# State-exchange attention and a squared-ReLU-like MLP in fp32 on one core: the last batch's state read placed later, and the states' outputs stored by two strided transfers per tile

## The chip, the cores and the metric

The kernel runs on one core of one Trainium2 chip. The metric is the device time of one execution in microseconds (us). A core has TensorE (PE: matmuls; its weight loads are listed as PEld), VectorE (DVE), ScalarE (ACT), GpSimd (POOL) and SyncE (SP). Transfers are issued here from the queues of SP and ACT and carried by 16 DMA engines. Matmul results land in PSUM, everything else on the chip is in SBUF, and both have 128 partitions.

## The reference

Eight batches of eight heads, 512 tokens and 32 states of 64 values each:

```
scores  = x @ state.T / 8;  xread = softmax(scores)  @ state    # tokens read the states
scores2 = state @ x.T / 8;  sread = softmax(scores2) @ x        # states read the tokens
rows = concat(xread, sread) per batch                           # 8 * (512 + 32) = 4352 rows of 512
h = rows @ w_in                                                 # 512 -> 2048
g = h if h >= 1, 0 if h <= -1, else (h + 1)**2 / 4
out = g @ w_out                                                 # 2048 -> 512, fp32
```

In `out`, batch b's rows are 544 b to 544 b + 543: first 512 token rows, then 32 state rows.

## The kernel before

Each matmul of the MLP is made of three: operands are split into a high and a low part, and high·high, low·high and high·low are summed in PSUM. The tokens of a batch never have their `xread` written out: the product of the states with `w_in` (called `sw`, fp32 matmuls, L385) is made per batch and per chunk of 256 of the 2048 hidden columns, so that the first layer is `softmax · sw` (L450 to L452, into PSUM tile `h`). ScalarE and VectorE turn `h` into `g` (L467 to L488), and L526 to L528 sum `g @ w_out` into four PSUM tiles `acc` of 128 tokens. After the start-up, whose order is a table of numbers, the program is a plain loop over `steps` (L812, L876): batches 1 to 7 with eight steps j each, and last a batch numbered 8, which is no batch of tokens but the 256 state rows of all eight batches (two `acc` tiles, four steps).

The change touches two places.

**The first step of a batch (j = 0), L880 to L895.** Behind the previous batch's last products stand, in PE's order: the states' read of the tokens (`read2`, L329: 32 matmuls at L337 into PSUM tile `sr`, from the transposed second softmax `e` and the tokens `xn`), then the `sw` products of seven chunks: 1 and 2 (into two `acc` banks), 3 and 4 (into the two `h` banks), 5 and 6 (two `acc` banks), and 7, for the last batch in the PSUM tile that `sr` uses. `scale2` (L342) is two VectorE operations: L345 normalises `sr` to `rs`, L349 transposes it to `rt`, which SP's queue puts in place for the last batch (L355, 16 small transfers). Then each pair of chunks is split: ScalarE casts the high part (L406, `copy` at L625), and VectorE subtracts to get the low part (L412). The first-layer product of step j = 1 takes chunk 1 and an `h` bank, and an `h` bank is free once the low part of the pair 3, 4 has been read from it.

**The end of the program, `store` (L534).** For batch 8, each `acc` tile t (0 and 1) holds 128 rows: 32 state rows of each of four batches. Tile 0 is copied to SBUF by ScalarE (L541), tile 1 by VectorE (L539). Then four transfers (L548) of 32 rows of 2 KB go out, one per batch, since in `out` the batches' state rows lie 544 rows apart; two are issued from ACT's queue and two from SP's. The last group of products is sorted by tile, so that tile 0's transfers go out while tile 1 is still being summed.

Of the kernel before, what the change touches and what calls it, by code (L numbers as in the profile page):

```python
# [98 lines left out]
def state_exchange_moe(  # L99
# [17 lines left out]
    nc = tc.nc  # L117
    B, P, NT, H, D = x.shape
    S = NT * P
    NS = 32  # L120
# [7 lines left out]
    TOK = S + NS  # L128
# [16 lines left out]
    def ps_mm(name):  # L145
        return ps.tile([P, 2, 512], F32, tag="mm", bufs=1, name=name)
# [30 lines left out]
    def load_xt(b):  # L177
        xt = work.tile([P, 2, NPR, S // 2], F32, tag="xt", bufs=1, name=f"xt{b}")
        for i in range(2):
            nc.sync.dma_start(out=xt[:, i], in_=xt_in[b, i])  # L180
        return xt

    def load_xn(b):
        xn = work.tile([P, NT, H, D], F32, tag="xn", bufs=1, name=f"xn{b}")
        nc.sync.dma_start(out=xn, in_=x[b])
        return [xn[:, t] for t in range(NT)]
# [12 lines left out]
    class Attention:  # L199
# [81 lines left out]
        def rest(self, q):  # L281
            nc.vector.tensor_tensor(
                out=self.atl[:, q], in0=self.zt[:, q], in1=self.ath[:, q].bitcast(F32), op=ALU.subtract
            )
# [76 lines left out]
    def split_tiles(name, home=None):  # L361
        if home:
            both = (rawp if home == "raw" else work).tile([P, 2, 1024], F32R, tag=home, bufs=2 if home == "raw" else 1, name=f"{name}hl")
            return both[:, 0], both[:, 1]
        hi = work.tile([P, 1024], F32R, tag="wh", name=f"{name}h")
        lo = work.tile([P, 1024], F32R, tag="wl", name=f"{name}l")
        return hi, lo
# [5 lines left out]
    def sw_product(items, apart=None, home=None):  # L373

        b, c = items[0]
        if apart:
            banks = [apart(f"sw{b}_{c}_{hh}") for hh in range(2)]
        else:
            pt = ps_mm(f"sw{b}_{c}")
            banks = [pt[:, hh] for hh in range(2)]  # L380
        for i, (bi, ci) in enumerate(items):
            for pr in range(NPR):
                for hh in range(2):
                    rows = slice(hh * 64, hh * 64 + 64)
                    nc.tensor.matmul(  # L385
                        banks[hh][pr * NS:(pr + 1) * NS, i * CI:(i + 1) * CI],
                        lhsT=sb[rows, bi, pr], rhs=w32[ci][rows, pr], start=True, stop=True,
                    )
        w = len(items) * CI
        if b == 0 and c < NH:  # L390
            whole = work.tile([P, 1024], F32, tag="wh", name=f"sw{b}_{c}w").rearrange("p (q f) -> p q f", q=2)[:, :, :w]
            sw_of[b, c] = [(banks[q][:, :w], whole[:, q], None) for q in range(2)]
            chunk[b, c] = whole, None
            return
        wh, wl = (
            v[:, :2 * w].rearrange("p (q f) -> p q f", q=2) for v in split_tiles(f"sw{b}_{c}", home)
        )
        if apart:
            sw_of[b, c] = [(banks[q][:, :w], wh[:, q], wl[:, q]) for q in range(2)]
        else:  # L400
            sw_of[b, c] = [(pt[:, :, :w], wh, wl)]
        for i, item in enumerate(items):
            cols = slice(i * CI, (i + 1) * CI)
            chunk[item] = wh[:, :, cols], wl[:, :, cols]

    def sw_high(b, c, engine="ACT"):  # L406
        for pt, wh, _ in sw_of[b, c]:
            copy(engine, wh, pt)

    def sw_low(b, c):  # L410
        for pt, wh, wl in sw_of[b, c]:
            nc.vector.tensor_tensor(out=wl, in0=pt, in1=wh.bitcast(F32), op=ALU.subtract)  # L412
# [9 lines left out]
    acc = {}  # L422
# [67 lines left out]
    def g1(b, j, split=True):  # L490
        hid = Hidden(b, j)
        for i in range(2):
            hid.product(i)
            hid.relu(i)
            hid.square(i)
            hid.bound(i)
            if i == 0:
                issue("half", b, j)
        if split:
            hid.high()  # L500
            hid.low()
        return hid

    def g2(b, j, half=None):
        n = n_of[b]
        per = S // n
        nt = n // P
        if b not in acc:
            acc[b] = [ps_acc(f"acc{b}_{t}") for t in range(nt)]
        gh, gl = gs[b, j]  # L510
        last = j == NJ // per - 1
        pairs = [(i, t) for i in range(2 * per) for t in range(nt)]
        if last:
            pairs.sort(key=lambda p: p[1])
        if half is not None:
            pairs = pairs[half * len(pairs) // 2:][:len(pairs) // 2]
        for i, t in pairs:
            f = 2 * per * j + i
            oh, ol = wo[f // 2][:, 0, f % 2], wo[f // 2][:, 1, f % 2]
            c0 = (i % per) * n + t * P  # L520
            lh, ll = (v if v is None else v[:, i // per, c0:c0 + P] for v in (gh, gl))
            a = acc[b][t]
            if ll is None:
                nc.tensor.matmul(a, lhsT=lh, rhs=ol, start=f == 0, stop=False)
                continue
            nc.tensor.matmul(a, lhsT=lh, rhs=oh, start=f == 0, stop=False)  # L526
            nc.tensor.matmul(a, lhsT=lh, rhs=ol, start=False, stop=False)  # L527
            nc.tensor.matmul(a, lhsT=ll, rhs=oh, start=False, stop=f == NF - 1)  # L528
            if last and i == 2 * per - 1:
                store(b, t)  # L530
# [3 lines left out]
    def store(b, t):  # L534
        if t == 0:
            outs[b] = rawp.tile([P, NT, DM], F32, tag="raw", name=f"o{b}")
        o = outs[b][:, t]
        if b == B and t % 2:
            nc.vector.tensor_copy(o, acc[b][t])  # L539
        else:  # L540
            nc.scalar.copy(out=o, in_=acc[b][t])  # L541
        if b < B:
            r0 = b * TOK + t * P
            nc.sync.dma_start(out=out[r0:r0 + P, :], in_=o)
        else:
            for i in range(4):
                r0 = (4 * t + i) * TOK + S
                (nc.sync if i % 2 else nc.scalar).dma_start(  # L548
                    out=out[r0:r0 + NS, :], in_=o[i * NS:(i + 1) * NS]
                )  # L550

# [67 lines left out]
    def copy(engine, out, src):  # L621
        if engine == "DVE":
            nc.vector.tensor_copy(out, src)
        else:
            nc.scalar.copy(out=out, in_=src)  # L625
# [28 lines left out]
    atts = {}  # L654

    def att_start(b, half=None):
        if half != 1:
            atts[b] = Attention(b)
        atts[b].scores(half)
# [138 lines left out]
    for word in GROUPS.split():  # L798
        c, n = word.split(".")
# [16 lines left out]
    def later(place, b, j, *items):  # L816
        for f, *a in items:
            background.setdefault((place, b, j), []).append((f, a))

    def issue(place, b, j):  # L820

        for f, a in background.get((place, b, j), ()):
            f(*a)
# [46 lines left out]
    for j in range(NJ // 2 - 1):  # L870
        later("half", B, j, (wi_split, 2 * j + 2))
        later("mid", B, j, (wi_split, 2 * j + 3))

    with guard:
        plan.emit(warm)
        for i, (b, j) in enumerate(steps):  # L876
            prior = steps[i - 1] if i else (0, NJ - 1)
            hid = g1(b, j, split=j or b == B)
            issue("mid", b, j)
            if j == 0 and b < B:  # L880
                g2(*prior, 0)
                hid.high()
                hid.low()
                g2(*prior, 1)
                atts[b].read2()
                sw_product([(b, 1), (b, 2)], ps_acc)
                sw_product([(b, 3), (b, 4)], ps_h)
                sw_product([(b, 5), (b, 6)], ps_acc, "xn")
                atts[b].scale2()
                if b + 1 < B:  # L890
                    att_start(b + 1)
                sw_product([(b, 7), (b + 1, 0)][:B - b], ps_acc if b + 1 < B else None, "raw")
                for c in (1, 3, 5, 7):
                    sw_high(b, c)
                    sw_low(b, c)  # L895
            else:
                g2(*prior)
            if j == 1 and b + 2 < B:
                loaded["xt", b + 2] = load_xt(b + 2)
            issue("end", b, j)  # L900
            if j == 6 and b + 1 < B:
                loaded["xn", b + 1] = load_xn(b + 1)
        g2(*steps[-1])
# [43 lines left out]
```

## Time and profile before

| | us |
|---|---|
| median of 3 runs | 640.0 (639.96 to 640.21) |
| the profiled execution's own time | 640.42 |
| its span, first to last instruction | 638.6 |
| PE busy in it | 628.7 |
| DVE / ACT busy in it | 359.6 / 370.1 |

The profiled execution took 0.4 us more than the median, and 1.8 us of its time lie outside the span. In the views, times are from the span's start. A line of a timeline gives start, length, engine, source line, operation, tiles written and read, and in brackets how long the engine was idle before and what ended that. "x2" and the like count instructions; an fp32 matmul of L337 or L385 shows as two. A DMA line on SPq or ACTq is the issuing, not the transfer; "to landing" is the time from issue to arrival.

### The profile page before, as it was taken

How to read it: one execution, taken by the hardware profiler on the slowest of the kernel's cores; microseconds unless marked ns; L12 is line 12 of the kernel's file. 1: busy time of each engine (PE TensorE's matmuls, PEld its weight loads, DVE VectorE, ACT ScalarE, POOL GpSimd, SP SyncE). 2: the span in 40 equal slices, each digit the busy share in tenths (PEclk: the TensorE clock that was granted, in tenths of full speed). 3: DMA queues.
4: the chain of work that ended last, by engine and by line, in shares of the span. 5: the costliest groups of instructions: out<-in, count | busy, mean ns of one | idle time of the engine just before them, and what ended most of it. 6: DMA issues, size and time to landing. Idle time of an engine off the chain costs nothing.

```text
span 638.6 us, 10431 instructions
## 1 busy us (share of the span) xinstructions
PE 628.7 (98%) x4286; PEld 505.0 (79%) x4286; DVE 359.6 (56%) x536; ACT 370.1 (58%) x539; POOL 0.8 (0%) x7
## 2 busy tenths in 40 slices
PE   7999999999999999999999999999999999999997
PEld 2577787888788887888788887888788878888896
DVE  5999957664565536553555536653555544335431
ACT  5999767545755556555755556555655555454641
POOL 0000000000000000000000000000000000000000
PEclk9999999999999999999999999999999999999999
DMA  8996022412222212011212112011202110000101
GB/s 328 422 371 229 13 70 84 107 28 69 70 69 30 73 50 88 9 26 67 70 67 34 67 67 72 12 32 57 71 1 34 66 69 5 0 1 1 66 1 33
DMA packets 52190, 48.38 MB, mean 76 GB/s; under 512 B 42288, under 2 KB 42416, under 8 KB 49200
## 3 DMA queue, kind: packets, MB, share of 16 engines
q1 hardware_dynamic: 51808, 47.40, 22.7%
q8 instruction: 33, 0.54, 0.4%
q10 hardware_dynamic: 336, 0.33, 0.2%
q14 instruction: 13, 0.11, 0.1%
HBM read 34.08 MB, written 8.91 MB: 67 GB/s over the span
## 4 chain that ended last, share of the span: by engine, by line
PE 89%; ACT 5%; DVE 3%; DMA 1%; issue 1%; SPq 0%; ACTq 0%; DVEq 0%
PE acc L526 18%; PE acc L528 18%; PE acc L527 18%; PE h L450 10%; PE h L451 10%; PE h L452 10%; PE sw L385 4%; PE sr L337 1%; DMA raw_i<-in_moe_w_in_dram 1%; ACT raw_i L580 1%; PE sc L227 1%; ACT raw_o L580 1%; DVE w L592 1%; ACT raw_i L572 1%; ACT u L467 1%
## 5 line engine op out<-in xcount | busy, mean ns | idle before, releaser
L526 PE MATMUL acc<-wo,gh 128*128 128x512 f32 x544 | 212.0, 390 | 0.0
L528 PE MATMUL acc<-wo,gl 128*128 128x512 f32 x544 | 211.8, 389 | 0.1
L527 PE MATMUL acc<-wo,gh 128*128 128x512 f32 x544 | 211.7, 389 | 0.0
L467 ACT ACTIVATE u<-h,half 128x512 f32<-128x512 f32 x136 | 93.3, 689 | 170.3 <-PE h L452 167.7
L474 DVE SCALAR_TENSOR_TENSOR u<-u,h 128x512 f32<-128x512 f32 x136 | 92.8, 687 | 169.0 <-ACT u L471 169.0
L488 DVE TENSOR_TENSOR gl<-u,gh 128x1024 fp32r<-128x1024 f32 x68 | 83.3, 1225 | 74.9 <-ACT gh L625 74.9
L526 PEld LDWEIGHTS acc<-wo,gh 128*128 128x128 f32 x544 | 102.1, 188 | 22.2 <-issue 1.2
L528 PEld LDWEIGHTS acc<-wo,gl 128*128 128x128 f32 x544 | 102.1, 188 | 22.0 <-DVE gl L488 0.7
L527 PEld LDWEIGHTS acc<-wo,gh 128*128 128x128 f32 x544 | 102.1, 188 | 21.1
L625 ACT CAST gh<-u 128x1024 fp32r<-128x1024 f32 x68 | 71.4, 1050 | 41.7 <-DVE u L474 41.6
L471 ACT ACTIVATE u<-u 128x512 f32<-128x512 f32 (+1 forms) x128 | 84.4, 660 | 4.0
L385 PE MATMUL sw<-w,sb 64*32 64x256 f32 x1024 | 32.2, 378 | 2.0 <-DVE w L592 2.0
L385 PEld LDWEIGHTS sw<-w,sb 64*32 64x32 f32 x1024 | 20.0, 106 | 12.9 <-DVE w L592 3.8
L541 ACT COPY o<-acc 128x512 f32<-128x512 f32 x33 | 19.1, 587 | 15.3 <-PE acc L528 15.3
L450 PE MATMUL h<-ath,sw_3h 128*128 128x512 f32 x64 | 25.0, 391 | 0.0
L452 PE MATMUL h<-atl,sw_3h 128*128 128x512 f32 x64 | 24.9, 389 | 0.0
L451 PE MATMUL h<-ath,sw_3l 128*128 128x512 f32 x64 | 24.9, 389 | 0.0
L450 PE MATMUL h<-ath,sw_1h 128*128 128x512 f32 x60 | 24.3, 404 | 0.5 <-DVE sw_3l L412 0.5
L451 PE MATMUL h<-ath,sw_1l 128*128 128x512 f32 x60 | 23.5, 392 | 0.0
L452 PE MATMUL h<-atl,sw_1h 128*128 128x512 f32 x60 | 23.3, 389 | 0.0
L450 PE MATMUL h<-ath,sw_5hl 128*128 128x512 f32 x56 | 21.8, 389 | 0.0
L451 PE MATMUL h<-ath,sw_5hl 128*128 128x512 f32 x56 | 21.8, 389 | 0.0
(174 smaller groups left out, 702.1 us busy)
## 6 DMA issues: line engine op xcount, KB each, us to landing
xt<-in_xt_dram SPq DMA_DIRECT2D x16, 512.0 KB, 4.2
raw_i<-in_moe_w_in_dram SPq DMA_DIRECT2D x8, 1024.0 KB, 7.7
raw_o<-in_moe_w_out_dram SPq DMA_DIRECT2D x8, 1024.0 KB, 10.6
out_dram<-o SPq DMA_DIRECT2D x32, 256.0 KB, 2.1
xn<-in_x_dram SPq DMA_DIRECT2D x7, 1024.0 KB, 4.9
e<-eb SPq DMA_DIRECT2D x112, 32.0 KB, 2.0
srT<-rt SPq DMA_DIRECT2D x128, 4.0 KB, 1.7
xn<-in_x_dram SPq DMA_DIRECT2D x2, 512.0 KB, 5.0
```

The source lines that it names most:

```text
L385: nc.tensor.matmul(banks[hh][pr * NS:(pr + 1) * NS, i * CI:(i + 1) * CI], lhsT=sb[rows, bi, pr], rhs=w32[ci][rows, pr], start=True, stop=True,
L450: nc.tensor.matmul(o, lhsT=wh[:, k, sl], rhs=ah[:, k], start=first, stop=False)
L451: nc.tensor.matmul(o, lhsT=wl[:, k, sl], rhs=ah[:, k], start=False, stop=False)
L452: nc.tensor.matmul(o, lhsT=wh[:, k, sl], rhs=al[:, k], start=False, stop=last)
L467: nc.scalar.activation(out=self.u[:, i], in_=self.hs[i], func=AF.Relu, scale=0.5, bias=half)
L471: nc.scalar.activation(out=u, in_=u, func=AF.Square)
L474: nc.vector.scalar_tensor_tensor(out=self.u[:, i], in0=self.u[:, i], scalar=1.0, in1=self.hs[i], op0=ALU.min, op1=ALU.max,)
L488: nc.vector.tensor_tensor(out=gl, in0=self.u, in1=gh.bitcast(F32), op=ALU.subtract)
L526: nc.tensor.matmul(a, lhsT=lh, rhs=oh, start=f == 0, stop=False)
L527: nc.tensor.matmul(a, lhsT=lh, rhs=ol, start=False, stop=False)
L528: nc.tensor.matmul(a, lhsT=ll, rhs=oh, start=False, stop=f == NF - 1)
L625: nc.scalar.copy(out=out, in_=src)
```

## The change

First, a new function `stretch(b)` holds the first step's `sw` work. For batches 1 to 6 it makes what stood there before. For batch 7 the read of the second softmax comes behind the products of the pairs 1, 2 and 3, 4; then the split of the pair 1, 2 is issued, then `scale2`, then the products of 5, 6 and 7, then the other splits. Second, batch 8's tiles are both copied by ScalarE, and each tile goes out in two transfers instead of four: each covers 64 rows of the SBUF tile, which are two batches of 32 rows in `out`, 544 rows apart. One is issued by ACT, one by SP.

```diff
-        if b == B and t % 2:
-            nc.vector.tensor_copy(o, acc[b][t])
-        else:
+        if b < B:
             nc.scalar.copy(out=o, in_=acc[b][t])
...
-        else:
-            for i in range(4):
-                r0 = (4 * t + i) * TOK + S
-                (nc.sync if i % 2 else nc.scalar).dma_start(
-                    out=out[r0:r0 + NS, :], in_=o[i * NS:(i + 1) * NS]
-                )
+            return
+
+        rows = out.rearrange("(b r) c -> b r c", r=TOK)[4 * t:4 * t + 4, S:S + NS]
+        nc.scalar.copy(out=o, in_=acc[b][t])
+        for i, queue in enumerate((nc.scalar, nc.sync)):
+            queue.dma_start(out=rows[2 * i:2 * i + 2], in_=o[2 * i * NS:2 * (i + 1) * NS])
...
+    def stretch(b):
+        def rest(*chunks):
+            for c in chunks:
+                sw_high(b, c)
+                sw_low(b, c)
+
+        final = b + 1 == B
+        if not final:
+            atts[b].read2()
+        sw_product([(b, 1), (b, 2)], ps_acc)
+        sw_product([(b, 3), (b, 4)], ps_h)
+        if final:
+            atts[b].read2()
+            rest(1)
+            atts[b].scale2()
+            sw_product([(b, 5), (b, 6)], ps_acc, "xn")
+            sw_product([(b, 7)], None, "raw")
+            rest(3, 5, 7)
+            return
...
-                atts[b].read2()
-                sw_product([(b, 1), (b, 2)], ps_acc)
-                sw_product([(b, 3), (b, 4)], ps_h)
-                sw_product([(b, 5), (b, 6)], ps_acc, "xn")
-                atts[b].scale2()
...
+                stretch(b)
```

On PE, in batch 7, the 32 matmuls of L337 move behind the 32 matmuls of the first two pairs. On VectorE, in the same place, this stood before (`rs` and `rt` are `scale2`'s tiles, `sw_1l` the low part of the pair 1, 2, `sw_3l` that of 3, 4, whose PSUM tiles are the `h` banks):

```order
L488 TENSOR_TENSOR gl_0_4689<-u_0_4650,gh_0_4688 128x1024
L345 TENSOR_TENSOR rs_4800<-sr_4708,r_7_4390 128x128
L349 STREAM_TRANSPOSE rt_4802<-rs_4800 128x128
L412 TENSOR_TENSOR sw_1l<-sw_1_0_4741,sw_1h 128x512
L412 TENSOR_TENSOR sw_1l<-sw_1_1_4742,sw_1h 128x512
L412 TENSOR_TENSOR sw_3l<-sw_3_0_4761,sw_3h 128x512
```

And this stands there now, on VectorE in the first step of batch 7:

```order
L412 TENSOR_TENSOR sw_1l<-sw_1_0_4708,sw_1h 128x512
L412 TENSOR_TENSOR sw_1l<-sw_1_1_4709,sw_1h 128x512
L345 TENSOR_TENSOR rs_4785<-sr_4748,r_7_4390 128x128
L349 STREAM_TRANSPOSE rt_4787<-rs_4785 128x128
L412 TENSOR_TENSOR sw_3l<-sw_3_0_4728,sw_3h 128x512
```

The two operations of `scale2` moved from ahead of the first pair's low parts to between the first pair and the second.

At the end of the program ScalarE's queue ended so before (`o` is the SBUF tile of the states' rows; the size behind a DMA is the shape that it counts through in `out`):

```order
L467 ACTIVATE u_3_5493<-h_3_1_5522,half 128x512
L471 ACTIVATE u_3_5493<-u_3_5493 128x512
L625 CAST gh_3_5550<-u_3_5493 128x1024
L541 COPY o_5590<-acc_0_5374 128x512
L548 DMA out_dram<-o_5590 32x512 x4
```

And ScalarE's queue ends so now:

```order
L622 CAST gh_3_5550<-u_3_5493 128x1024
L545 COPY o_5590<-acc_0_5374 128x512
L547 DMA out_dram<-o_5590 2x32x512
L545 COPY o_5590<-acc_1_5375 128x512
L547 DMA out_dram<-o_5590 2x32x512
L955 UNCONDITIONAL_BRANCH
```

Each tile's two transfers of 32x512 on this queue became one of 2x32x512, with the copy of the second tile between them; on SP's queue, likewise, four transfers of 32x512 became two of 2x32x512.

More of the change, by code (lines that the diff above doesn't have):

```diff
@@ L537, in store @@
         o = outs[b][:, t]
-        if b == B and t % 2:
-            nc.vector.tensor_copy(o, acc[b][t])
-        else:
+        if b < B:
             nc.scalar.copy(out=o, in_=acc[b][t])
-        if b < B:
             r0 = b * TOK + t * P
             nc.sync.dma_start(out=out[r0:r0 + P, :], in_=o)
-        else:
-            for i in range(4):
-                r0 = (4 * t + i) * TOK + S
-                (nc.sync if i % 2 else nc.scalar).dma_start(
-                    out=out[r0:r0 + NS, :], in_=o[i * NS:(i + 1) * NS]
-                )
+            return
[3 more added lines that the diff above has]
+            queue.dma_start(out=rows[2 * i:2 * i + 2], in_=o[2 * i * NS:2 * (i + 1) * NS])
     raws = {}
@@ L872, in state_exchange_moe @@
         later("mid", B, j, (wi_split, 2 * j + 3))
+    def stretch(b):
[16 more added lines that the diff above has]
+            return
+        sw_product([(b, 5), (b, 6)], ps_acc, "xn")
+        atts[b].scale2()
+        att_start(b + 1)
+        sw_product([(b, 7), (b + 1, 0)], ps_acc, "raw")
+        rest(1, 3, 5, 7)
     with guard:
@@ L884, in state_exchange_moe @@
                 g2(*prior, 1)
-                atts[b].read2()
-                sw_product([(b, 1), (b, 2)], ps_acc)
-                sw_product([(b, 3), (b, 4)], ps_h)
-                sw_product([(b, 5), (b, 6)], ps_acc, "xn")
-                atts[b].scale2()
[L890 to L895, printed above, removed]
+                stretch(b)
             else:
```

## The prediction

> **What bounds the kernel now.** I read the page first, then the chain of waits around the two places of the change, then the timelines, the stage table and the transfers there. The page says that TensorE is busy nearly all the time and makes most of the chain that ended last:
>
> ```profile
> span 638.6 us, 10431 instructions
> PE 628.7 (98%) x4286; PEld 505.0 (79%) x4286; DVE 359.6 (56%) x536; ACT 370.1 (58%) x539; POOL 0.8 (0%) x7
> PE 89%; ACT 5%; DVE 3%; DMA 1%; issue 1%; SPq 0%; ACTq 0%; DVEq 0%
> ```
>
> So time can be won or lost only where PE waits, or after its last product. The chain in batch 7's first step (start, length, what) shows such a wait:
>
> ```profile
> 522.04 1.03 PE sr L337 x64
> 523.08 1.13 PE sw L385 x32
> 524.21 0.57 ACT sw_1h L625
> ...
> 524.81 1.29 DVE sw_1l L412 x2
> 526.10 0.61 DVE sw_3l L412
> 526.71 0.04 issue
> 526.75 0.50 PE h L450
> ```
>
> PE's products of the pair 1, 2 come behind the read `sr`; ScalarE and VectorE split that pair, and PE's next first-layer product starts at 526.75, when the first `h` bank has been read for `sw_3l`. PE's and VectorE's rows of the same stretch:
>
> ```profile
> 521.97 0.94 PEld L337 LDWEIGHTS sr<-xn,e 128*32 128x32 f32 x64 [0.35 <-issue]
> 521.98 1.10 PE L337 MATMUL sr<-xn,e 128*32 128x64 f32 x64
> 523.00 3.25 PE L385 MATMUL sw<-w,sb 64*32 64x256 f32 x112
> 523.14 0.29 DVE L345 TENSOR_TENSOR rs<-sr,r 128x128 f32<-128x128 f32 x1 [0.99 <-PE sr L337]
> 523.55 0.31 DVE L349 STREAM_TRANSPOSE rt<-rs 128x128 f32<-128x128 f32 x1
> ```
>
> PE's own work there ends at 523.00 + 3.25 = 526.25, so it idles 0.50 us. The other place is the end: copies, issues, and the stage table (its last columns: granted clock, share of the 16 DMA engines, GB/s).
>
> ```profile
> 632.46 0.38 ACTq L548 DMA_DIRECT2D out_dram<-o  x1
> 634.56 0.69 DVE L539 COPY o<-acc 128x512 f32<-128x512 f32 x1 [6.49 <-PE acc L528]
> 635.28 0.78 SPq L548 DMA_DIRECT2D out_dram<-o  x2
> 635.28 0.85 ACTq L548 DMA_DIRECT2D out_dram<-o  x2
> ```
>
> ```profile
> 632.40:633.20 0.80, 0.80 (x5) 0.68 (x4) 0.00 (x0) 0.03 (x1) 0.00 (x0) 1.00 0.00 0
> 633.20:634.80 1.60, 1.32 (x6) 0.75 (x4) 0.24 (x1) 0.00 (x0) 0.00 (x0) 1.00 0.66 164
> 634.80:635.90 1.10, 0.00 (x0) 0.00 (x0) 0.45 (x1) 0.00 (x0) 0.00 (x0) 1.00 0.00 0
> 635.90:637.30 1.40, 0.00 (x0) 0.00 (x0) 0.00 (x0) 0.00 (x0) 0.00 (x0) 1.00 0.74 187
> 637.30:638.60 1.30, 0.00 (x0) 0.00 (x0) 0.00 (x0) 0.00 (x0) 0.00 (x0) 0.71 0.00 0
> ```
>
> Tile 0's packets move in the second stage and are gone before tile 1's start; tile 1's fill the fourth stage; then 1.3 us pass with no packet until the span ends. From the last product (634.5) to the end, 4.1 us lie open, under no other work: whatever the transfers cost more is added in full.
>
> **The change, part one: the later read.** Nothing is removed or added, 64 records of L337 trade places with 32 + 32 of L385. The pair 1, 2 starts where `sr` started, 521.98 instead of 523.00: everything to the end of `sw_1l` moves 1.02 earlier, to 526.10 − 1.02 = 525.08. Now `scale2` follows on VectorE. Its input: `sr` now starts behind two pairs, 64 of the 112 records of L385, so 3.25 × 64/112 = 1.86 later, at 523.84, and L345 followed `sr`'s start by 523.14 − 521.98 = 1.16, which gives 525.00. It is ready when `sw_1l` ends. From L345's start to L349's end were 523.55 + 0.31 − 523.14 = 0.72; so `sw_3l` starts at 525.80 and PE at 525.80 + 0.61 + 0.04 = 526.45 instead of 526.75: **0.30 saved**. Queued behind `scale2` on VectorE are the low parts of 3, 5 and 7; SP's 16 small transfers (L355) go 1.9 later, but nothing waits for them before batch 7's step 6, so they cost nothing. PE's tile for chunk 7 is `sr`'s, free at 525.08 + 0.29 = 525.37, before PE comes to it at 525.79. Not in this trace is a switch from L385 to L337. Bounds: the row above has 0.35 of issue ahead of L337; paid once more it eats the gain, paid on both sides of the moved read it costs 0.2. At best PE is free only at 526.25, which saves 0.5. I take 0.30, with −0.2 to 0.5.
>
> **Part two: the copy.** ScalarE's copy instead of VectorE's saves 0.1:
>
> ```profile
> 631.84 0.59 ACT L541 COPY o<-acc 128x512 f32<-128x512 f32 x1 [5.03 <-PE acc L528]
> ```
>
> It stands behind tile 0's issue on ScalarE's queue, and that is over long before 634.5.
>
> **Part three: the transfers, on which all hangs.** How is a transfer dealt out to the 16 engines? Two windows, one holding one whole 256 KB transfer of L544 in 1.0 us, the other the four 64 KB ones of tile 1 in 1.4 us:
>
> ```profile
> DMA packets 144, 0.26 MB, mean 262 GB/s; under 512 B 16, under 2 KB 16, under 8 KB 144
> ## 3 DMA queue, kind: packets, MB, share of 16 engines
> q1 hardware_dynamic: 144, 0.26, 69.9%
> ```
>
> ```profile
> DMA packets 192, 0.26 MB, mean 187 GB/s; under 512 B 64, under 2 KB 64, under 8 KB 192
> ...
> q10 hardware_dynamic: 96, 0.13, 41.2%
> q1 hardware_dynamic: 96, 0.13, 32.8%
> ```
>
> One transfer has one packet for each 2 KB row (128, and 4 × 32) and 16 small ones: 16 shares, each closed by one, of 8 rows or of 2. In both, as in every transfer that the program writes, the SBUF side and the other side begin with the same count, 128 or 32, which 16 divides. The new transfer is the first whose sides differ: 64 rows in SBUF, 2 batches of 32 rows in `out`, so that its outermost count is 2. If shares are cut along the outermost counts, as 8 of 128 and 2 of 32 are, there are only two shares, 32 rows of 2 KB for each of two engines. A generator that walked the rows instead would still give 16. The trace can't show which; I hold the first far likelier, because a share that needs one start address and one step on each side can't otherwise be cut from both shapes alike.
>
> The Trainium skill, "DMA: Bandwidth & Descriptors", section "Why a DMA increments its semaphore by 16 and not by 1", states this as a rule: the transfer runs on the largest number of engines up to 16 that divides the slowest dimension that isn't 1 on both sides, and they are the lowest-numbered ones; its "Rules for kernel authors" warn of an outermost dimension under 16. By that rule 64 and 2 give 2 engines, the same two for both queues, and the sum is the 647.1 below; without it, 639.5. The transfers of the windows above used 16, in agreement with it, and no run so far shows it at another number.
>
> Price of a packet: the first window has 0.699 × 16 × 1.0 = 11.2 us of engine time for 128 rows, 0.087 us a row; the second 0.740 × 16 × 1.4 = 16.6, 0.13 a row. The two tiles have 256 rows together; on two engines that is 128 rows each, **11.2 us at the first price, 16.6 at the second**. I take the first: with 2 of 16 engines at work less can collide, and the second comes where two queues drew on all 16.
>
> When it starts: tile 0's first packet in this row (40 slices of 0.05 us from 633.0) is in the sixth slice, 633.3, 0.84 after its issue.
>
> ```profile
> DMA  0000019589559796945969699944100000000000
> L325 SPq DMA_DIRECT2D e<-eb x112: 597/609/1604, 74.4 to 491.9; - x112
> ```
>
> A three-dimensional transfer (L325) took 0.61 to issue against 0.38 here, so 0.23 is added; two bounds, 0 and 0.23. Tile 1's transfers are issued at about 634.54 − 0.3 + 0.6 = 634.9, while tile 0's 64 rows per engine last from 633.2 until 638.8, so the engines don't run dry: the copy's 0.1 and the fewer issues are hidden behind tile 0's packets and win nothing.
>
> Sum in the profiled execution: 633.3 − 0.3 + 0.23 + 11.2 = 644.4 for the last packet, + 1.3 = 645.7 against 638.6: **+7.1**. The profiled execution took 640.42 and the median is 640.0; the same +7.1 on the median gives **647.1**. Bounds: 633.3 − 0.5 + 11.2 + 1.3 = 645.3, +6.7, 646.7; and 633.3 + 0.2 + 0.23 + 16.6 + 1.3 = 651.6, +13.0, 653.0.
>
> **The rivals.** *All 16 engines still share each transfer* (ends on the other side, not slower). For it: 16 shares in both windows, and 64 rows of 2 KB would divide by 16. Against: the two sides no longer count alike. Then tile 1's packets, which came 0.84 after an issue at 635.28, start at 636.12 − 0.1 − 0.3 + 0.23 = 635.95, and 16 engines need 11.2/16 = 0.7 to 16.6/16 = 1.04: last packet 636.65 to 637.0, against 637.3. That is 0.3 to 0.65 saved, 639.35 to 639.7, say 639.5; if the moved read costs 0.2 instead, about 640.0. The change decides between it and my forecast at the number of shares alone: from 8 engines up, tile 1's 128 rows at 0.087 take at most 1.4 us, what they fill in the fourth stage above, and nothing is lost.
>
> *Two shares, but SP's and ACT's queues land on different pairs of engines.* For it: nothing here says where the dealing starts. Against: both queues' shares came on the same 16 so far. Four engines take 64 rows each, 5.6 us: 633.23 + 5.6 + 1.3 = 640.1, +1.5, 641.5.
>
> *The later read wins nothing*, because of the issue ahead of L337: it moves each of these by 0.3 to 0.5 and decides no sign.
>
> **How the numbers follow.** Two engines: 0.82. Four: 0.05. Sixteen: 0.13. 0.2% of 640.0 is 1.3 us, about what a measurement can tell from no change. The two- and four-engine cases are slower by more: 0.87. The sixteen-engine case is within it, except for 0.02 that it gains more than its rows allow: same 0.11, faster 0.02. The likeliest is 647.1, its own range 646.7 to 653.0. The range reaches down just past the four-engine case, to 641.4, and leaves out the sixteen.
>
> **What would show it.** Right: transfers of L547 that take 6 us and more to land; after the last product a DMA share near 2/16 = 0.125 for some 10 us, at 2 × 2 KB / 0.087 us = 47 GB/s; 2 small packets for each of the four transfers instead of 16; in batch 7 the first-layer product at 526.45, and `scale2` between the two low parts. Wrong: a landing within about 2 us and 16 small packets each, with the end near 638; or a DMA share near 4/16. A share at 0.125 that lasts 14 us would say that the mechanism holds and the row's price is the second one.

## The result, and the profile after

The changed kernel takes 648.93 us (median of 4 runs, 648.8 to 649.32) against 640.11 for the kernel before beside it: 1.0134 times as long, 95% interval 1.0121 to 1.0146, some 8.8 us slower. Its profiled execution took 649.32, with a span of 647.5 against 638.6: 8.9 us more.

First the end of the program, where nearly all of that lies. The timeline of the changed kernel there (start, length, engine, line; for a DMA line the length is the issuing):

```profile
632.26 3.29 SPq L547 DMA_DIRECT2D out_dram<-o  x2
632.26 1.38 ACTq L547 DMA_DIRECT2D out_dram<-o  x1
...
634.37 0.58 ACT L545 COPY o<-acc 128x512 f32<-128x512 f32 x1 [2.13 <-PE acc L528]
634.98 0.52 ACTq L547 DMA_DIRECT2D out_dram<-o  x1
```

And its stage table from tile 0's first packet to the last instruction (last three columns: granted clock, share of the 16 DMA engines, GB/s):

```profile
633.50:637.00 3.50, 0.83 (x4) 0.36 (x2) 0.00 (x0) 0.58 (x1) 0.00 (x0) 1.00 0.12 28
637.00:638.00 1.00, 0.00 (x0) 0.00 (x0) 0.00 (x0) 0.00 (x0) 0.00 (x0) 0.55 0.14 37
638.00:646.30 8.30, 0.00 (x0) 0.00 (x0) 0.00 (x0) 0.00 (x0) 0.00 (x0) 0.50 0.12 47
646.30:647.50 1.20, 0.00 (x0) 0.00 (x0) 0.00 (x0) 0.00 (x0) 0.00 (x0) 0.50 0.00 0
```

The last product ends at 634.3, 0.2 earlier than before; but packets move until 646.3 instead of 637.3. The share stands at 0.12 to 0.14 throughout: two engines of sixteen are 0.125. The packets of these 12.8 us say the same:

```profile
DMA packets 264, 0.52 MB, mean 41 GB/s; under 512 B 8, under 2 KB 8, under 8 KB 264
## 3 DMA queue, kind: packets, MB, share of 16 engines
q1 hardware_dynamic: 132, 0.26, 6.9%
q10 hardware_dynamic: 132, 0.26, 5.5%
```

256 rows and 8 small packets for four transfers, so two shares each, where the kernel before closed each transfer with 16.

Second, the chain of waits of the changed kernel in batch 7's first step:

```profile
522.02 0.23 PE acc L528
522.24 1.89 PE sw L385 x64
524.13 1.03 PE sr L337 x64
525.16 1.46 PE sw L385 x48
526.62 0.45 PE h L450
```

PE has the whole chain; ScalarE's and VectorE's pieces have left it. From the last product ahead of the stretch to the first-layer product are 526.62 − 522.02 = 4.60 us. Before, that last product stands in the chain at 521.82 and the first-layer product at 526.75, 4.93: 0.33 saved. VectorE's and the weight loads' rows of the same stretch:

```profile
523.98 1.29 DVE L412 TENSOR_TENSOR sw_1l<-sw,sw_1h 128x512 fp32r<-128x512 f32 x2 [1.62 <-ACT sw_1h L622]
525.23 0.29 DVE L345 TENSOR_TENSOR rs<-sr,r 128x128 f32<-128x128 f32 x1
525.63 0.31 DVE L349 STREAM_TRANSPOSE rt<-rs 128x128 f32<-128x128 f32 x1
525.87 1.25 DVE L412 TENSOR_TENSOR sw_3l<-sw,sw_3h 128x512 fp32r<-128x512 f32 x2
```

```profile
524.06 0.94 PEld L337 LDWEIGHTS sr<-xn,e 128*32 128x32 f32 x64 [0.41 <-issue]
526.57 0.19 PEld L450 LDWEIGHTS h<-ath,sw_1h 128*128 128x128 f32 x1 [0.44 <-DVE sw_3l L412]
```

`scale2` fills the gap between the two pairs, with no idle time of VectorE ahead of it. The weight loads of L337 have 0.41 us of issue ahead of them, but PE's own chain runs on there without a gap. At the end PE's own products (L385, until 526.62 in the chain) and VectorE's release by `sw_3l` (526.57) come within 0.05 us of each other: the wait that the change shortens is used up, and a still earlier release would win nothing.

### The profile page after: what moved, and what is told of

The parts are those of the page before. It is cut to its first block, busy times and chain, and to the rows that moved or that the text cites. A ratio compares the mean times of both kernels' runs of the same rounds, so it can differ in the third digit from the quotient of the medians.

```text
span 647.5 us, 10427 instructions
## 1 busy us (share of the span) xinstructions
PE 628.6 (97%) x4286; PEld 505.2 (78%) x4286; DVE 358.9 (55%) x535; ACT 370.7 (57%) x540; POOL 0.8 (0%) x7
## 4 chain that ended last, share of the span: by engine, by line
PE 89%; ACT 5%; DVE 3%; DMA 1%; issue 1%; SPq 0%; ACTq 0%; DVEq 0%
PE acc L526 18%; PE acc L527 18%; PE acc L528 18%; PE h L450 10%; PE h L451 10%; PE h L452 9%; PE sw L385 4%; PE sr L337 1%; DMA raw_i<-in_moe_w_in_dram 1%; ACT raw_i L577 1%; PE sc L227 1%; ACT raw_o L577 1%; DVE w L589 1%; ACT raw_i L569 1%; ACT u L467 1%
## 5 line engine op out<-in xcount | busy, mean ns | idle before, releaser
L385 PE MATMUL sw<-w,sb 64*32 64x256 f32 x1024 | 32.3, 379 | 2.2 <-DVE w L589 2.1
L385 PEld LDWEIGHTS sw<-w,sb 64*32 64x32 f32 x1024 | 19.8, 106 | 13.2 <-DVE w L589 3.9
L452 PE MATMUL h<-atl,sw_5hl 128*128 128x512 f32 x56 | 21.8, 390 | 0.0
L451 PE MATMUL h<-ath,sw_5hl 128*128 128x512 f32 x56 | 21.8, 390 | 0.0
```

The lines of the kernel that those rows point to most:

```text
L385: nc.tensor.matmul(banks[hh][pr * NS:(pr + 1) * NS, i * CI:(i + 1) * CI], lhsT=sb[rows, bi, pr], rhs=w32[ci][rows, pr], start=True, stop=True,
L451: nc.tensor.matmul(o, lhsT=wl[:, k, sl], rhs=ah[:, k], start=False, stop=False)
L452: nc.tensor.matmul(o, lhsT=wh[:, k, sl], rhs=al[:, k], start=False, stop=last)
```

## The experiments

My theory: the loss is the number of shares, and a transfer gets as many as the largest number up to 16 that divides the outermost counts of both its sides. Rivals: a strided, three-dimensional transfer is slow by itself; or the later read carries part of the loss. Times of the kernel before beside these runs are 640.38 and 640.39.

**The later read alone.** The changed kernel with the old `store`.

> The later read alone, with the stores of before. If the loss is in the transfers alone: the first-layer product of batch 7's step 1 starts 0.3 to 0.4 us earlier relative to the last product ahead of the stretch, and the time falls by about 0.35, to 639.7. If the later read carries part of the loss: above 640.3.

639.76 us, ratio 0.9991 (0.9982 to 1.0). The read is no part of the loss. The trace shows the step; the time shows no more than its direction, at the edge of what can be told. The chain of waits of this kernel:

```profile
521.53 0.23 PE acc L528
521.76 1.89 PE sw L385 x64
523.65 1.03 PE sr L337 x64
524.68 1.46 PE sw L385 x48
526.13 0.45 PE h L450
```

Again 4.60 us from row to row, as in the changed kernel.

**The stores alone.** The kernel before with the new `store`.

> The new stores and ScalarE's copy alone, with the read where it was. If the loss is in the transfers alone: 0.35 above the whole change, about 649.2. If the read carries part of it: below 648.5.

649.51, ratio 1.0142 (1.0128 to 1.0156). The transfers, with ScalarE's copy, make the whole loss.

**Four batches in one transfer.** The outermost count doubled to 4, still strided:

```diff
-        for i, queue in enumerate((nc.scalar, nc.sync)):
-            queue.dma_start(out=rows[2 * i:2 * i + 2], in_=o[2 * i * NS:2 * (i + 1) * NS])
+        nc.sync.dma_start(out=rows, in_=o)
```

> One transfer per tile, from SP's queue, over all four batches: 128 rows in SBUF, 4 batches of 32 rows in out, so that the outermost count is 4. If shares are cut along the outermost counts: 4 engines with 64 rows each over both tiles, 5.6 us at 0.087 a row or 6.4 at the 0.1 that the changed kernel showed; last packet near 639.5, time 641.9 to 642.6, and 4 small packets per transfer. If a transfer over several strided blocks is slow by itself, whatever its outermost count: as slow as the change, 648 or more.

644.31, ratio 1.006 (1.0046 to 1.0073): 3.9 us are lost, less than half of the 8.8, and four engines instead of two are at work. The packets of this kernel from 632.4 to 642.4 (the first row's 40 slices are of 0.25 us), and its stage:

```profile
DMA  0004313002312222222231232222111100000000
...
DMA packets 264, 0.52 MB, mean 52 GB/s; under 512 B 8, under 2 KB 8, under 8 KB 264
```

```profile
633.00:641.20 8.20, 0.85 (x4) 0.38 (x2) 0.00 (x0) 0.58 (x1) 0.00 (x0) 0.76 0.22 64
```

8 small packets for two transfers are four shares each, and a share of 0.22 is close under 4/16. But 8.2 us for 64 rows per engine is more than the 5.6 to 6.4 that I expected, so the time came out some 2 us above; the next section returns to that.

**Sixteen rows outermost.** The states' columns are reordered where they are split, so that a tile holds 16 state rows of all eight batches; the transfer is strided and three-dimensional as before.

```diff
-        src = srT.rearrange("p a b n -> p a (b n)")
-        nc.vector.tensor_copy(sh, src)
-        nc.vector.tensor_tensor(out=sl, in0=src, in1=sh.bitcast(F32), op=ALU.subtract)
+        src = srT.rearrange("p a b n -> p a n b")
+        hi, lo = (v.rearrange("p a (n b) -> p a n b", b=B) for v in (sh, sl))
+        nc.vector.tensor_copy(hi, src)
+        nc.vector.tensor_tensor(out=lo, in0=src, in1=hi.bitcast(F32), op=ALU.subtract)
...
-        rows = out.rearrange("(b r) c -> b r c", r=TOK)[4 * t:4 * t + 4, S:S + NS]
+        rows = out.rearrange("(b r) c -> r b c", r=TOK)[S + 16 * t:S + 16 * t + 16]
...
+        nc.sync.dma_start(out=rows, in_=o)
```

> The states' columns are put in the order row, batch when they are split, so that a tile holds 16 state rows of all 8 batches; one transfer per tile from SP's queue steps over 16 rows and, inside, 8 batches: still strided and three-dimensional, 128 rows in SBUF, outermost count 16. If shares are cut along the outermost counts: 16 shares, tile 1's 128 rows in about 0.7 us, landing within 2.5 us, time 639.2 to 639.7. If the strided form is slow by itself: 648 or more.

640.39, ratio 1.0002 (0.9993 to 1.0011). The strided form without the small outermost count costs none of the 8.8 us. It is also not the 639.2 to 639.7 that I expected. The timeline has tile 1's issue,

```profile
634.43 0.58 SPq L546 DMA_DIRECT2D out_dram<-o  x1
```

and these are its packets, from 634.4 in slices of 0.1 us:

```profile
DMA  0000000000005498949898841000000000000000
...
DMA packets 144, 0.26 MB, mean 66 GB/s; under 512 B 16, under 2 KB 16, under 8 KB 144
```

16 shares, but the first packet comes in the thirteenth slice, 1.2 us after the issue.

**Eight outermost.** The same order of columns, each tile in two transfers of eight rows by eight batches, one from each queue.

> As e4_rows_first, but each tile in two transfers of 8 rows by 8 batches, one from ScalarE's queue and one from SP's: 64 rows in SBUF, outermost count 8. Shares by the outermost counts: 8 engines take 16 rows each of a tile, 1.35 us at the 84 ns that most packets took and 2.0 at 124, against 1.27 in e4_rows_first; 0.1 to 0.7 above e4_rows_first, and 8 small packets per transfer. If 64 rows from two queues were dealt to 16 engines: not above e4_rows_first. If ScalarE's packets come late as they did in the changed kernel (4.6 us after their issue): over 2 us above it.

641.02, ratio 1.0008 (0.9999 to 1.0017), 0.6 above the run before it: within the expectation, though the two intervals overlap. Its packets over both tiles:

```profile
DMA packets 288, 0.52 MB, mean 82 GB/s; under 512 B 32, under 2 KB 32, under 8 KB 288
```

32 small packets for four transfers: eight shares each.

**One queue.** The changed kernel with all four transfers from SP.

> The changed kernel with all four transfers of 64 rows from SP's queue, none from ScalarE's. Shares by the outermost counts: still two engines with 128 rows each, so slow as before within 2 us. If the overlong packets of the first tile (160 ns a row and engine against 84) come of two queues meeting on the two engines: 128 x 0.084 = 10.8 us instead of 12.7, time near 647.0. If a strided transfer begins so by itself: 648.5 to 649.5. If the two queues used different engines: twice the stream, 655 and more.

648.59, ratio 1.0132 (1.0118 to 1.0145). Its stage from first to last packet:

```profile
633.10:645.80 12.70, 0.85 (x4) 0.38 (x2) 0.00 (x0) 0.58 (x1) 0.00 (x0) 0.63 0.12 41
```

12.7 us against 12.8, so the two queues use the same two engines, and their meeting isn't what makes the stream longer than 11.2. Nor does the second queue win anything. All packets of this stream stand on q1, which is therefore SP's queue:

```profile
q1 hardware_dynamic: 264, 0.52, 12.1%
```

In the changed kernel the packets from 632.2 to 636.2 are SP's alone:

```profile
q1 hardware_dynamic: 38, 0.08, 9.1%
```

So no packet of the transfer that ACT issued at 632.26 begins within 3.9 us of its issue. Why it waits is not shown.

**The change without its strided transfers.** The later read and ScalarE's copy, four plain transfers per tile; the lines are shown against the kernel with the later read alone.

```diff
-        if b == B and t % 2:
-            nc.vector.tensor_copy(o, acc[b][t])
-        else:
-            nc.scalar.copy(out=o, in_=acc[b][t])
+        nc.scalar.copy(out=o, in_=acc[b][t])
```

> The later read and ScalarE's copy of both tiles, with the four plain transfers per tile of before: the change without its strided transfers. 0.1 under e1_read_only, that is 0.4 to 0.7 under the kernel before, about 639.7. If ScalarE's issues stand in the way of its copy: not under e1_read_only.

639.79, ratio 0.9991 (0.9982 to 1.0001): the same as the later read alone. The copy's 0.1 doesn't show in the time. Of all kernels here these two are the fastest, and neither is clear of the kernel before. Tile 1's issues on SP's queue in the timeline, and the packets from 634.7 in slices of 0.1 us:

```profile
634.75 0.78 SPq L545 DMA_DIRECT2D out_dram<-o  x2
```

```profile
DMA  0000000058959938999300000000000000000000
```

The first packet comes in the ninth slice, 0.8 after the first issue, and the last in the twentieth, 2.0 after it; in the kernel with sixteen rows outermost the last came 2.5 after its one issue (634.43 to the twenty-fifth slice, 636.9).

**31 rows.** The one test with nothing strided and less moved. Against the kernel just above, each transfer leaves out the last state row of its batch:

```diff
-                    out=out[r0:r0 + NS, :], in_=o[i * NS:(i + 1) * NS]
+                    out=out[r0:r0 + NS - 1, :], in_=o[i * NS:(i + 1) * NS - 1]
```

> As e7_read_and_copy, but each of the eight plain transfers carries 31 of its 32 rows: the last state row of each batch is left out. Nothing is strided or three-dimensional, and less is moved. 31 is prime. Shares by the outermost count: one engine takes each transfer, the same for all, 248 rows x 0.084 = 20.8 us from the first packet on; time near 656, and 1 small packet per transfer. If only the strided form is slow: 639.5 to 640.5.

657.03 us in one run. Its packets and stages:

```profile
DMA packets 256, 0.51 MB, mean 24 GB/s; under 512 B 8, under 2 KB 8, under 8 KB 256
```

```profile
632.50:637.00 4.50, 1.40 (x7) 0.82 (x5) 0.00 (x0) 0.58 (x1) 0.00 (x0) 1.00 0.06 17
637.00:653.90 16.90, 0.00 (x0) 0.00 (x0) 0.00 (x0) 0.00 (x0) 0.00 (x0) 0.56 0.07 25
```

Eight transfers, eight small packets, a share of 0.06 to 0.07, which is 1/16: one engine carries all, at 25 GB/s. Leaving out one row of 32 made the kernel 16.6 us slower than the kernel before. A strided form is thus not needed for a loss, and with sixteen rows outermost it did not make one. With 1, 2, 4, 8 and 16 shares seen for outermost counts of 31, 2, 4, 8 and 16 (the other side 31, 64, 128, 64 and 128), the rule of the Trainium skill, "DMA: Bandwidth & Descriptors", section "Why a DMA increments its semaphore by 16 and not by 1", agrees in each. The counts tried are powers of two and one prime, so a rule that took only powers of two would have given the same shares; no run here tells the two apart.

## Why the prediction was right, and where its size was off

The case forecast as the likeliest is what happened: two engines. By its steps:

- **The later read.** Forecast 0.30 saved, measured 0.33 in the chain; with the read alone the time is 0.6 lower, interval 0 to 1.2. The forecast ready time of `scale2`, the end of `sw_1l`, held: the row at 525.23 has no wait. The issue ahead of L337, my bound on the other side, shows in the weight loads' row (0.41) and not in PE's chain: PE's own stretch took 4.38 us (522.24 to 526.62) instead of 4.27 (521.98 to 526.25), and so ended only 0.05 from VectorE's release.
- **The copy.** Forecast hidden. In the kernels where it is not, it doesn't show either (639.79 against 639.76).
- **The shares.** Two, as forecast, at both queues the same: 8 small packets, a share of 0.12 to 0.14, and one queue as long as two.
- **The price of a row.** 0.087 us held for the later part: 47 GB/s in the stage from 638.0 on are 2 × 2 KB in 0.087 us. It did not hold ahead of that: 28 and 37 GB/s in the first 4.5 us. The stream took 12.8 us instead of 11.2; this term was mis-sized by 1.6. The reason given for the choice of this price, that the second came of two queues on all 16 engines, did not hold either. With sixteen rows outermost, one queue alone paid the second: the row below is its stage with tile 1's packets, 0.72 × 16 × 1.4 / 128 = 0.13 us a row. That the first price came near was therefore partly luck.

```profile
635.60:637.00 1.40, 0.00 (x0) 0.00 (x0) 0.00 (x0) 0.00 (x0) 0.00 (x0) 0.71 0.72 187
```

- **The first packet.** Forecast for 633.2, that is 1.07 after an issue at 632.16; it came at about 633.5, 1.25 after the issue at 632.26:

```profile
DMA  0000000000000110400020310001111111200104
GB/s 0 0 0 0 0 0 0 0 0 0 0 0 0 41 20 20 41 0 20 0 20 0 20 20 0 20 20 41 41 41 61 41 61 41 61 20 20 41 20 41
```

(The packets of the changed kernel from 632.2 in slices of 0.1 us, each counted in the slice in which it begins: the first is in the fourteenth.) This is 0.3 more.

- **The tail.** 1.2 without a packet, against 1.3 forecast.

Sum: +7.1 forecast, + 1.6 + 0.3 − 0.1 = +8.9, as the spans have it. The time lies between the two prices that bounded it, 647.1 and 653.0.

What makes the first packets long is not settled. The engines are counted busy all the while: a share of 0.12 at 28 GB/s is, for rows of 2.048 KB, 16 × 0.12 × 2.048 / 28 = 0.14 us a row, and the same working gives 0.08 for the stage from 638.0 on. In the GB/s row above, 20 is one row begun in a slice: until 634.9 there are at most two and in four slices none, then two or three, and from 635.7 again one or two. The meeting of two queues isn't needed for it, since one queue has it too. Nor is the strided form: the plain transfers of 31 rows moved 17 GB/s until 637.0 and 25 after that. At four shares, 64 rows per engine took 8.2 instead of 5.6 us. It doesn't only follow an issue, either. These are the packets of the kernel with one queue from 633.0, in slices of 0.325 us:

```profile
GB/s 19 25 6 13 32 44 50 50 38 38 50 44 57 50 50 50 50 50 50 50 50 44 44 32 19 0 50 44 50 50 50 50 50 57 50 50 50 25 25 0
```

The rate is low until 634.3 and falls again at 640.5 to 641.4, some 4 us after SP's last issue had ended (636.3). And the plain 256 KB transfer of the prediction's first window shows nothing of it, at 0.087 us a row over all its rows.

The rival of sixteen shares was priced too low: 639.5 forecast, 640.39 in the kernel that has them. The strided transfer's first packet comes 0.4 later than a plain one's (1.2 against 0.8 after the issue), and the last one 0.5 later (2.5 against 2.0), which is about the 0.6 between these two kernels' times. The other difference of that kernel, the reordered split on VectorE (L841: 2.09 us instead of 1.23), doesn't show at the end: its tile 1 is issued at 634.43, no later than the 634.75 of the plain one. So this edit had nothing to win here, with all sixteen engines either.

## What to carry to other kernels

Before merging transfers, write down the outermost count of both sides as the instruction carries them: a rearranged view that puts a small batch count outermost leaves the transfer to that many engines, and where it stands last, the whole of it is added to the time. The small closing packets in the profile's packet counts (16 per transfer or fewer) and the DMA share (here 0.125 and 0.06) show it at a glance, in every run. One row left out of 32 cost more here (16.6 us) than the strided view (8.8).

## What had not been expected

- With 31 rows per transfer the program was slower than with any strided form: 657.03 us, one engine, in the end at 25 GB/s.
- A strided, three-dimensional transfer with all 16 shares has its first packet 1.2 us after the issue, against 0.8 for a plain one.
- The mean granted clock of the changed kernel is 0.992 instead of 0.999. That is no throttling of its work: the stages show 1.00 until 637.0 and 0.50 to 0.55 only where PE had been idle for 2.7 us and more.
